# Program order of batches 0 to 2 redone, and zero matmuls of up to 512 columns in place of several of 128

## The chip, the cores and the metric

The kernel runs on one core of a Trainium2 chip. The metric is the device time of one execution in microseconds (us). A profiled execution has a span some 1.8 us shorter than its timed value; spans are compared with spans only.

## The reference

A retention layer (attention without softmax, with a decay by distance) feeds a two-layer network with the tanh form of GELU. There are 8 batches, 8 heads, 576 positions and 64 values a head; the network is 512 by 2048 by 512 over 4608 tokens.

```python
def _attn_ref(q, k, v):
    scale = 1.0 / np.sqrt(D_)
    scores = scale * np.matmul(q, k.transpose(0, 1, 3, 2))
    gamma = 1.0 - 2.0 ** (-5.0 - np.arange(H))
    Dmat = np.where(rel >= 0, gamma[:, None, None] ** rel[None], 0.0)   # rel = i - j
    return np.matmul(scores * Dmat[None], v)

def _moe_ref(x, w_in, w_out):
    h = x @ w_in
    g = 0.5 * h * (1.0 + np.tanh(c * (h + 0.044715 * h * h * h)))
    return g @ w_out
# ... x is the retention output, transposed to (tokens, heads * values)
```

## The kernel before

The retention is worked out in chunks of 128 positions, two to a "pair" of chunks. For each (batch, pair, head half) the kernel loads fp32 tiles of q, k and v, casts them to fp16, transposes q and k on TensorE (`tr`), makes scores (`score_mm`), masks them on VectorE (`mask_sc`), transposes a rescaled key back (`back`), makes the state of the chunk (`state_mm`), carries it along on VectorE (`scan`), casts it (`put`), and adds inner and carried parts in PSUM, the banks that TensorE's products are written to (`values`, `inter_mm`), which `evac` writes as the input of the network. `up` and `up_half` make the first network product; `down` makes the second.

```python
    def tr(b, s, hh, i, eng):                 # q or k: four PE transposes, then a copy
        a = att[b]
        t = bank("tr", F16)
        pad(("tr", b, s, hh, i), t)
        for g in range(4):
            nc.tensor.transpose(t[:, 128 * g : 128 * g + 128], a["kq"][:, s, hh, i, 128 * g : 128 * g + 128], ident)
        # ... copies to a["T"] by eng; S2 means half on ScalarE, half on VectorE

    def back(b, s, hh, eng):
        # ... four transposes of a["T"] into t
        copy(eng, a["kq"][:, s, hh, 0, :], t[:, 0:512])

    def put(b, n, eng, hhs=(0, 1)):           # two casts of a state
        # ...
        for hl in range(2):
            e = (A, V)[hl] if eng is S2 else eng
            copy(e, tbd[b % 2][half[hl], n, qs, half[hl]], w[half[hl], qs])
```

Zero matmuls are put ahead of real ones. Their products are never used, since the real matmul that follows overwrites the bank; they keep TensorE from standing still.

```python
    def pad(key, t, o=0):
        for _ in range(pads.pop(key, 0)):
            if t.dtype == F16:
                nc.tensor.transpose(t[:, 0:128], wz[:, 0:128], ident)
            else:
                nc.tensor.matmul(t[:, o : o + 128], wz[:, 0:128], wz[:, 0:128], start=(o == 0), stop=True, skip_group_check=True)
```

The order of all this is fixed by hand. `units` is a list of 79 pieces of work for batches 0 to 2: units 0 to 9 are empty, 10 on are the network's products. `plan` lists (unit, step) pairs; after each unit its steps are emitted in the order of the list. Each engine gets its own instructions in that order, so a step that stands early on an engine holds up all later ones of that engine. In both kernels q and k of batch 0 are cast to a layout of four-token tiles (the set `R4`), so this is not part of the difference.

```python
    def run(units, plan):
        for i, f in enumerate(units):
            f()
            for step in plan.get(i, ()):
                step()
    # ...
    units = [L(int) for _ in range(10)] + [L(F0.up_half, j, 1) for j in (0, 1)] + [L(int)] * 2 + [L(F0.up, f) for f in range(4, NF)]
    units += [L(F1.up_half, j, u) for u in range(2) for j in range(NJ)]
    units += [L(F.down, m) for F in (F0, F1) for m in MS]
    units += [L(F2.up, f) for f in range(NF)] + [L(F2.down, m) for m in MS]
    plan = add({},
        # ...
        (5, L(put, 0, 1, A)),                 # state cast on ScalarE
        # ...
        (6, L(put, 0, 0, A)),                 # state cast on ScalarE
        # ...
        (7, L(back, 0, 1, 1, A)),             # the kq copy that the second half of the state product waits for
        # ...
        (6, L(cast_w_in, 0, 3, A)),           # weight cast on ScalarE, unit 6: ahead of back in unit 7
        # ...
    )
```

Of the kernel before, what the change touches and what calls it, by code (L numbers as in the profile page):

```python
# [12 lines left out]
F32 = mybir.dt.float32  # L13
# [6 lines left out]
def kernel(  # L20
# [124 lines left out]
    def pad(key, t, o=0):  # L145
        for _ in range(pads.pop(key, 0)):
            if t.dtype == F16:
                nc.tensor.transpose(t[:, 0:128], wz[:, 0:128], ident)
            else:
                nc.tensor.matmul(t[:, o : o + 128], wz[:, 0:128], wz[:, 0:128], start=(o == 0), stop=True, skip_group_check=True)  # L150
# [140 lines left out]
    def load_w_in(g, ct, home=None):  # L291
        load_w(("i", g, ct), moe_w_in[128 * ct : 128 * ct + 128, 512 * g : 512 * g + 512], home)
# [592 lines left out]
    def add(plan, *entries):  # L885
# [16 lines left out]
    load_qkv(0, 0, 1, "q", None)  # L902
    load_qkv(0, 1, 1, "q", None)
    load_qkv(0, 1, 1, "k", None)
    load_qkv(0, 0, 1, "v", None)
    load_qkv(0, 0, 0, "v", None)
    load_w_in(0, 3, E)
    load_qkv(0, 1, 0, "v", None)
    load_qkv(0, 1, 1, "v", None)
    load_w_in(0, 2, E)  # L910
    load_w_in(0, 1, E)
    load_w_in(0, 0, E)
    load_w_in(1, 1, E2)
    load_w_in(1, 0, E2)
    load_w_in(1, 3, E2)
    load_w_in(2, 1, None)
    load_w_in(2, 2, None)
    load_qkv(1, 0, 0, "k", None)
    load_w_in(1, 2, E2)
    load_qkv(1, 0, 1, "q", None)  # L920
# [3 lines left out]
    load_qkv(1, 0, 1, "k", None)  # L924
    load_qkv(1, 0, 0, "v", None)
    load_w_in(3, 3, None)
    load_w_in(3, 1, None)
    load_w_in(3, 2, None)
    load_w_in(3, 0, None)
    load_qkv(1, 0, 1, "v", None)  # L930
    load_qkv(1, 1, 1, "q", O)
    load_qkv(1, 1, 0, "q", O)
    load_qkv(1, 1, 0, "k", O)
    load_qkv(1, 1, 1, "k", O)
    load_w_out(0, None)
    load_qkv(1, 1, 0, "v", O)
    load_qkv(1, 1, 1, "v", O)
    load_w_out(1, None)
    load_w_out(6, E3)
    load_w_out(2, None)  # L940
    load_w_out(4, E3)
    load_w_out(3, None)
    load_w_out(5, E3)
    load_w_out(14, H)
    load_w_out(8, O)
    load_w_out(10, H)
    load_w_out(7, E3)
    load_w_out(12, H)
    load_w_out(9, O)
    load_w_out(11, H)  # L950
    load_w_out(15, H)
    load_qkv(2, 1, 1, "q", None)
    load_qkv(2, 1, 0, "k", None)
    load_w_out(13, H)
    load_qkv(2, 0, 0, "q", None)
    load_qkv(2, 0, 0, "k", None)
    load_qkv(2, 1, 0, "q", None)
    load_qkv(2, 0, 0, "v", None)
    load_qkv(2, 0, 1, "q", None)
    load_qkv(3, 0, 1, "k", None)  # L960
    load_qkv(2, 0, 1, "v", None)
    load_qkv(2, 0, 1, "k", None)
    load_qkv(2, 1, 1, "k", None)
    load_qkv(2, 1, 1, "v", None)
    load_qkv(2, 1, 0, "v", None)
    load_tail(0)
    load_qkv(3, 0, 0, "q", None)
    load_qkv(3, 0, 0, "v", None)
# [8 lines left out]
    load_qkv(3, 1, 1, "q", None)  # L977
    load_tail(2)
    load_qkv(3, 1, 1, "v", None)


    pads.update({
        ("tr", 0, 1, 0, 0): 8,
        ("tr", 0, 1, 1, 0): 0,
        ("tr", 0, 1, 1, 1): 0,
        ("st", 0, 1, 0): 1,
        ("st", 0, 1, 1): 8,
# [4 lines left out]
        ("us", 0, 0): 2,  # L992
        ("us", 0, 1): 8,
        ("xs", 0, 0): 5,
        ("xs", 0, 1): 0,
        ("in", 0, 3): 0,
        ("tr", 0, 0, 0, 0): 7,
        ("tr", 0, 0, 0, 1): 11,
# [5 lines left out]
        ("tr", 0, 1, 0, 1): 6,  # L1004
        ("in", 0, 1): 10,
# [8 lines left out]
    def turn():  # L1014
# [8 lines left out]
        (0, L(cast_qk, 0, 0, 0, "q", A)),  # L1023
        (0, L(cast_qk, 0, 0, 0, "k", V)),
        (1, L(new_x, 0)),
        (0, L(cast_qk, 0, 1, 0, "q", V)),
        (0, L(tr, 0, 0, 0, 0, V)),
        (0, L(cast_qk, 0, 1, 0, "k", A)),
        (0, L(mask)),
        (1, L(tr, 0, 0, 0, 1, V)),  # L1030
        (1, L(tr, 0, 1, 0, 0, V)),
        (2, L(score_mm, 0, 0, 0)),
        (2, L(mask_sc, 0, 0, 0)),
        (2, L(back, 0, 0, 0, V)),
        (1, L(tr, 0, 1, 0, 1, S2)),
        (3, L(score_mm, 0, 1, 0)),
        (0, L(cast_qk, 0, 0, 1, "k", A)),
        (2, L(cast_qk, 0, 0, 1, "q", G)),
        (3, L(back, 0, 1, 0, A)),
        (3, L(tr, 0, 1, 1, 1, V)),  # L1040
        (2, L(tr, 0, 0, 1, 0, S2)),
        (2, L(tr, 0, 0, 1, 1, A)),
        (1, L(cast_qk, 0, 1, 1, "q", G)),
        (3, L(mask_sc, 0, 1, 0)),
        (5, L(back, 0, 0, 1, A)),
        (1, L(cast_qk, 0, 1, 1, "k", G)),
        (3, L(tr, 0, 1, 1, 0, A)),
        (4, L(score_mm, 0, 0, 1)),
        (4, L(mask_sc, 0, 0, 1)),
        (5, L(state_mm, 0, [0])),  # L1050
        (3, L(cast_v, 0, 0, 0, G)),
        (5, L(scan, 0, 0)),
        (3, L(cast_v, 0, 0, 1, G)),
# [3 lines left out]
        (6, L(mask_sc, 0, 1, 1)),  # L1057
# [3 lines left out]
        (7, L(back, 0, 1, 1, A)),  # L1061
        (8, L(inter_mm, 0, 0, 1)),
        (8, L(evac, 0, 0, 1)),
        (7, L(cast_v, 0, 1, 1, V)),
        (7, L(cast_v, 0, 1, 0, G)),
        (5, L(evac, 0, 0, 0)),
        (7, L(state_mm, 0, [1])),
        (7, L(scan, 0, 2)),
        (7, L(put, 0, 2, S2)),
        (8, L(inter_mm, 0, 1, 1)),  # L1070
        (8, L(inter_mm, 0, 1, 0)),
        (7, L(values, 0, 1)),
        (9, L(cast_w_in, 0, 2, G)),
        (9, L(evac, 0, 1, 0)),
# [4 lines left out]
        (6, L(cast_w_in, 0, 3, A)),  # L1079
        (8, L(cast_w_in, 0, 1, G)),  # L1080
        (8, L(cast_w_in, 0, 0, G)),
        (12, L(put, 0, 3, A)),
        (9, L(F0.up_half, 0, 0)),
# [4 lines left out]
        (7, L(cast_w_in, 1, 0, A)),  # L1088
        (10, L(cast_w_in, 2, 1, A)),
        (7, L(cast_w_in, 1, 3, A)),  # L1090
        (12, L(F0.mix_sc, 0, 2, V)),
        (8, L(cast_w_in, 1, 1, A)),
        (9, L(cast_w_in, 2, 2, V)),
        (7, L(turn)),
        (12, L(F0.mix_sa, 0, 2, V)),
        (9, L(cast_w_in, 2, 0, V)),
        (7, L(cast_w_in, 1, 2, A)),
        (19, L(F0.mix_sc, 2, 2, V)),
        (17, L(cast_qk, 1, 0, 1, "q", V)),
        (10, L(cast_qk, 1, 0, 0, "q", A)),  # L1100
        (18, L(F0.mix_d, 0, 2, V)),
        (15, L(tr, 1, 0, 0, 0, S2)),
        (18, L(cast_w_in, 3, 0, A)),
        (19, L(tr, 1, 0, 1, 1, A)),
        (15, L(tr, 1, 0, 1, 0, V)),
        (19, L(F0.mix_sa, 2, 2, G)),
        (19, L(score_mm, 1, 0, 0)),
        (22, L(mask_sc, 1, 0, 1)),
        (17, L(cast_w_in, 3, 2, G)),
# [3 lines left out]
        (21, L(cast_v, 1, 0, 1, G)),  # L1113
        (19, L(cast_w_in, 3, 1, A)),
        (20, L(F0.mix_d, 2, 2, V)),
        (21, L(new_x, 1)),
        (20, L(cast_v, 1, 0, 0, G)),
        (19, L(mask_sc, 1, 0, 0)),
        (21, L(score_mm, 1, 0, 1)),
        (22, L(state_mm, 1, [0])),  # L1120
        (14, L(cast_w_in, 3, 3, G)),
        (24, L(cast_qk, 1, 1, 0, "k", V)),
# [3 lines left out]
        (27, L(cast_qk, 1, 1, 1, "q", A)),  # L1126
        (22, L(values, 1, 0)),
        (29, L(put, 1, 1, A)),
        (21, L(cast_qk, 1, 1, 0, "q", A)),
        (25, L(cast_v, 1, 1, 0, V)),  # L1130
        (25, L(tr, 1, 1, 0, 0, V)),
        (27, L(F0.mix_sc, 4, 2, G)),
        (23, L(evac, 1, 0, 1)),
        (22, L(evac, 1, 0, 0)),
        (24, L(cast_qk, 1, 1, 1, "k", A)),
        (26, L(cast_v, 1, 1, 1, V)),
        (28, L(tr, 1, 1, 1, 1, A)),
        (24, L(F0.mix_sa, 4, 2, V)),
        (27, L(tr, 1, 1, 0, 1, A)),
# [3 lines left out]
        (30, L(mask_sc, 1, 1, 0)),  # L1143
        (31, L(mask_sc, 1, 1, 1)),
        (28, L(score_mm, 1, 1, 0)),
        (29, L(score_mm, 1, 1, 1)),
        (32, L(inter_mm, 1, 1, 1)),
        (29, L(scan, 1, 2)),
        (29, L(put, 1, 2, A)),
        (30, L(mix_w_out, 0, "sums", G)),  # L1150
        (31, L(values, 1, 1)),
        (31, L(mix_w_out, 0, "sub", V)),
        (41, L(mix_w_out, 3, "add", G)),
        (31, L(inter_mm, 1, 1, 0)),
        (28, L(mix_w_out, 1, "copy", A)),
        (33, L(mix_w_out, 1, "add", G)),
        (33, L(mix_w_out, 2, "sums", G)),
        (32, L(mix_w_out, 1, "sums", G)),
        (33, L(evac, 1, 1, 1)),
        (32, L(mix_w_out, 3, "sub", V)),  # L1160
        (32, L(evac, 1, 1, 0)),
        (33, L(mix_w_out, 2, "add", V)),
        (41, L(mix_w_out, 7, "add", V)),
        (37, L(mix_w_out, 3, "sums", V)),
        (37, L(mix_w_out, 3, "copy", A)),
        (37, L(mix_w_out, 1, "sub", V)),
        (35, L(mix_w_out, 0, "copy", A)),
        (33, L(mix_w_out, 2, "copy", A)),
        (36, L(mix_w_out, 0, "add", V)),
        (36, L(mix_w_out, 4, "sums", G)),  # L1170
        (34, L(mix_w_out, 2, "sub", V)),
        (37, L(mix_w_out, 6, "sums", V)),
        (43, L(mix_w_out, 4, "add", G)),
# [384 lines left out]
```

## Time and profile before

| | before |
|---|---|
| time, median of 4 runs (range) | 301.67 us (301.43 to 303.33) |
| span of the profiled execution | 299.3 us |
| instructions; matmuls of TensorE | 8979; 3775 |
| TensorE busy | 289.3 us (97%) |
| first network product (`hp`, 256 columns) | 24.45 us |

Timelines give start, duration, engine, line and operation, with the idle time of the engine just before in brackets and what ended it. I use four marks on TensorE's timeline in all kernels, since between them the same work is done: the first `hp` product of 256 columns (start of the network of batch 0), the first `my` product (its second layer), the first `hp` product of batch 2, and the first `my` product of batch 3. For the kernel before they stand at 24.45, 59.73, 92.75 and 143.02 us, and TensorE ends at 295.93. The stretches between the first three marks hold units 10 to 55; the last stretch holds units 56 to 78 and the first network product of batch 3. This table by stretch of the kernel before has the columns: stretch, length, busy time (instructions) of TensorE, its weight loads, VectorE, ScalarE and GpSimd, then granted clock, DMA share, GB/s.

```profile
24.45:59.73 35.28, 34.76 (x447) 24.97 (x445) 31.45 (x58) 31.49 (x69) 22.29 (x21) 1.00 0.96 287
59.73:92.75 33.02, 32.97 (x574) 28.30 (x572) 31.33 (x62) 18.70 (x40) 13.73 (x18) 1.00 0.82 206
92.75:143.02 50.27, 49.48 (x708) 30.54 (x707) 41.97 (x80) 31.26 (x60) 17.35 (x20) 1.00 0.95 233
```

The reader is to see the difference between length and TensorE's busy time: 0.52, 0.05 and 0.79 us. All three stretches are bound by TensorE; 1.36 us is all that can be won after the start.

### The profile page before, as it was taken

What the parts mean: (1) busy time and instruction counts of PE and PEld (TensorE: products, weight loads), DVE (VectorE), ACT (ScalarE), POOL (GpSimd) and SP (SyncE); (2) the same over time, 40 slices, a digit from 0 to 9 for tenths busy, and PEclk for the clock granted to TensorE, in tenths of its full rate; (3) what the DMA queues carried; (4) which work ended last, traced back from release to release, by engine and by line L of the source; (5) the groups of instructions that cost most, each with busy time, mean ns of one, the idle gap of its engine ahead of it and who ended that gap; (6) DMA issues with size and microseconds to landing.
All of it is one profiled execution on the core that took longest, in us unless ns stands there. A gap on an engine that the chain in (4) does not pass through costs nothing.

```text
span 299.3 us, 8979 instructions
## 1 busy us (share of the span) xinstructions
PE 289.3 (97%) x3775; PEld 210.3 (70%) x3775; DVE 234.4 (78%) x450; ACT 167.9 (56%) x328; POOL 97.5 (33%) x128
## 2 busy tenths in 40 slices
PE   7879999999999999999999999999999999999995
PEld 6757467888886558745875587558754886787684
DVE  3786989989998897798567756799778298886774
ACT  7448969984474782465535653565445317614830
POOL 4651687545240054084035104699100000000000
PEclk9999999999999999999999999999999999999999
DMA  6998999659979999996997799663030003002204
GB/s 219 336 358 263 313 375 313 182 139 227 231 223 206 264 285 173 273 310 103 194 291 219 106 198 282 193 120 39 8 136 1 2 0 143 0 2 70 72 0 140
DMA packets 92663, 52.48 MB, mean 175 GB/s; under 512 B 38352, under 2 KB 86480, under 8 KB 92624
## 3 DMA queue, kind: packets, MB, share of 16 engines
q1 hardware_dynamic: 92288, 51.26, 64.7%
q10 hardware_dynamic: 336, 0.66, 0.8%
q8 instruction: 29, 0.48, 0.7%
q14 instruction: 10, 0.08, 0.1%
HBM read 36.70 MB, written 9.44 MB: 154 GB/s over the span
## 4 chain that ended last, share of the span: by engine, by line
PE 81%; DVE 8%; ACT 7%; DMA 2%; issue 1%; SPq 0%; DVEq 0%; ACTq 0%
PE hp L635 26%; PE my L777 10%; PE mz L777 9%; PE mu L777 5%; PE mv L777 5%; PE mw L777 5%; PE hp L721 5%; ACT tbd L241 2%; PE py L665 2%; DVE ret L445 2%; PE xs L574 2%; PE xs L547 2%; PE st L432 2%; DMA ld<-in_q_dram 2%; ACT gT L639 1%; DVE ws L520 1%
## 5 line engine op out<-in xcount | busy, mean ns | idle before, releaser
L635 PE MATMUL hp<-x,w_in_sb 128*128 128x512 f16 x400 | 92.1, 379 | 0.6 <-ACT gT L639 0.5
L639 ACT ACTIVATE gT<-hp 128x512 f16<-128x512 f32 x108 | 63.6, 596 | 42.2 <-PE hp L635 41.5
L635 PEld LDWEIGHTS <-w_in_sb 128*128 128x128 f16 x432 | 40.9, 98 | 43.5 <-issue 1.0
L777 PEld LDWEIGHTS <-gT 128*128 128x128 f16 x576 | 55.8, 98 | 8.1 <-ACT gT L708 0.2
L445 DVE TENSOR_TENSOR ret<-st,cm 128x512 f16<-128x512 f32 x64 | 40.0, 681 | 4.1 <-PE st L432 4.1
L241 POOL CAST kq<-ld 128x512 f16<-128x512 f32 x26 | 20.8, 801 | 64.7 <-DMA ld<-in_k_dram 32.2
L241 ACT CAST tbd<-ws 64x256 f16<-64x256 f32 x63 | 25.4, 403 | 24.4 <-DVE ws L520 23.8
L254 POOL TENSOR_TENSOR cv<-ld,sc 128x512 f16<-128x512 f32 x28 | 30.2, 1090 | 26.6 <-DMA ld<-in_v_dram 22.7
L777 PE MATMUL my<-w_out_sb,gT 128*128 128x256 f16 x288 | 34.5, 273 | 0.0
L777 PE MATMUL mz<-w_out_sb,gT 128*128 128x256 f16 x288 | 34.4, 273 | 0.0
L777 PEld LDWEIGHTS <-gsum 128*128 128x128 f16 x288 | 27.9, 98 | 3.4
L746 DVE TENSOR_TENSOR gsum<-gT 128x1024 f16<-128x1024 f16 x35 | 28.0, 800 | 2.2 <-ACT gT L727 1.7
L750 DVE TENSOR_TENSOR gT<-gT 128x1024 f16<-128x1024 f16 x36 | 27.7, 787 | 0.1
L587 DVE TENSOR_TENSOR x<-xs,gx 128x512 f16<-128x512 f32 x32 | 21.7, 684 | 5.5 <-PE xs L574 5.3
L804 DVE TENSOR_TENSOR ost<-ost,mv 128x512 f32<-128x512 f32 x18 | 11.6, 683 | 13.5 <-issue 9.4
L738 DVE TENSOR_TENSOR gdia<-gT 128x512 f16<-128x512 f16 (+1 forms) x33 | 18.0, 544 | 4.9 <-ACT gT L708 2.5
L721 PE MATMUL hp<-x,w_in_sb 128*128 128x256 f16 x160 | 18.7, 273 | 0.0
L241 ACT CAST kq<-ld 128x512 f16<-128x512 f32 x28 | 17.0, 616 | 2.5 <-DMA ld<-in_k_dram 1.3
L777 PE MATMUL mu<-w_out_sb,gsum 128*128 128x256 f16 x144 | 17.2, 273 | 0.0
L777 PE MATMUL mv<-w_out_sb,gsum 128*128 128x256 f16 x144 | 17.2, 273 | 0.0
L777 PE MATMUL mw<-w_out_sb,gdia 128*128 128x256 f16 x144 | 17.2, 273 | 0.0
L721 PEld LDWEIGHTS <-w_in_sb 128*128 128x128 f16 x160 | 15.2, 98 | 1.9
(117 smaller groups left out, 393.1 us busy)
## 6 DMA issues: line engine op xcount, KB each, us to landing
ld<-in_k_dram SPq DMA_DIRECT2D x30, 256.0 KB, 5.1
ld<-in_q_dram SPq DMA_DIRECT2D x30, 256.0 KB, 5.3
ld<-in_v_dram SPq DMA_DIRECT2D x30, 256.0 KB, 5.4
out_dram<-ost SPq DMA_DIRECT2D x14, 512.0 KB, 4.3
loan<-in_moe_w_out_dram SPq DMA_DIRECT2D x12, 256.0 KB, 5.4
loan<-in_moe_w_in_dram SPq DMA_DIRECT2D x8, 256.0 KB, 6.1
ld<-in_moe_w_in_dram SPq DMA_DIRECT2D x8, 256.0 KB, 6.1
ld<-in_moe_w_out_dram SPq DMA_DIRECT2D x4, 256.0 KB, 6.5
```

The source lines that it names most:

```text
L241: (eng.copy if eng is nc.scalar else eng.tensor_copy)(out=out, in_=in_)
L254: eng.tensor_tensor(out=unperm(att[b]["v"][:, s, hh, :]), in0=perm(t), in1=sc[:, 8 * hh : 8 * hh + 8] .rearrange("p (r h) -> p r h", r=2) ...
L445: nc.vector.tensor_tensor(out=x.rearrange("p (a m) -> p a m", a=2), in0=st[hl].rearrange("p (a m) -> p a m", a=2), in1=cm.rearrange("p r s ...
L587: nc.vector.tensor_tensor(out=xb[b][:, :, 2 * s + c].rearrange("p s q i -> p q s i"), in0=att[b]["x", s][c].rearrange("p (q s i) -> p q s ...
L635: nc.tensor.matmul(hp, w_in_sb[:, ct, 128 * f : 128 * f + 128], x[:, :, ct, :], start=(ct == 0), stop=(ct == 3),)
L639: nc.scalar.activation(out=self.g(f // 2)[:, f % 2], in_=hp, func=AF.Gelu_apprx_tanh)
L721: nc.tensor.matmul(hp[:, 256 * h : 256 * h + 256], w_in_sb[:, ct, 256 * j + 128 * h : 256 * j + 128 * h + 128], xb[self.b][:, :, 2 * u : 2 ...
L738: e.tensor_tensor(out=self.sa[:, j : j + n], in0=g[:, :, 0, 0:256], in1=g[:, :, 1, 256:512], op=ALU.add)
L746: e.tensor_tensor(out=self.sc[:, j : j + n], in0=g[:, :, 0], in1=g[:, :, 1], op=ALU.add)
L750: e.tensor_tensor(out=g.rearrange("p j h c -> p j (h c)")[:, :, 256:768].rearrange("p j (h c) -> p j h c", h=2), in0=g[:, :, :, 0:256], in ...
L777: nc.tensor.matmul(t[u] if isinstance(t, list) else t[:, 256 * u : 256 * u + 256], lhs(j, slice(128 * u, 128 * u + 128)), w_out_sb[:, j, w ...
L804: nc.vector.tensor_tensor(out=out, in0=in0, in1=t, op=op)
```

## The change

The intent: fewer waits in the first 25 us by another order of the steps on each engine, smaller corrections of order later, and nearly the same columns of zero matmuls (132 units of 128 columns for 127) in fewer instructions. The core of the diff (cut):

```diff
     def pad(key, t, o=0):
-        for _ in range(pads.pop(key, 0)):
-            if t.dtype == F16:
-                nc.tensor.transpose(t[:, 0:128], wz[:, 0:128], ident)
-            else:
-                nc.tensor.matmul(t[:, o : o + 128], wz[:, 0:128], wz[:, 0:128], start=(o == 0), stop=True, skip_group_check=True)
+        n = pads.pop(key, 0)
+        t = t.bitcast(F32) if t.dtype == F16 else t
+        while n > 0:
+            m = min(n, (512 - o) // 128)
+            nc.tensor.matmul(
+                t[:, o : o + 128 * m],
+                wz[:, 0:128],
+                wz[:, 0:128].unsqueeze(1).to_broadcast([128, m, 128]),
+                start=(o == 0), stop=True, skip_group_check=True,
+            )
+            n -= m
 # ... loads in another order
-    load_qkv(0, 1, 1, "q", None)
     load_qkv(0, 1, 1, "k", None)
+    load_qkv(0, 1, 1, "q", None)
 # ... zero matmuls in units of 128 columns, e.g.
-        ("st", 0, 1, 1): 8,
+        ("st", 0, 1, 1): 12,
-        ("us", 0, 1): 8,
+        ("us", 0, 1): 4,
 # ... start
-        (3, L(back, 0, 1, 0, A)),
-        (3, L(tr, 0, 1, 1, 1, V)),
-        (2, L(tr, 0, 0, 1, 0, S2)),
-        (2, L(tr, 0, 0, 1, 1, A)),
+        (3, L(tr, 0, 1, 1, 1, S2)),
+        (2, L(back, 0, 1, 0, A)),
+        (1, L(tr, 0, 0, 1, 0, S2)),
+        (3, L(tr, 0, 0, 1, 1, A)),
-        (7, L(cast_v, 0, 1, 1, V)),
+        (6, L(cast_v, 0, 1, 1, G)),
-        (6, L(cast_w_in, 0, 3, A)),
+        (7, L(cast_w_in, 0, 3, A)),
-        (12, L(put, 0, 3, A)),
+        (11, L(put, 0, 3, V)),
-        (7, L(cast_w_in, 1, 0, A)),
+        (7, L(cast_w_in, 1, 0, V)),
 # ... some 150 further moves of (unit, step) pairs up to unit 78, such as
-        (24, L(F0.mix_sa, 4, 2, V)),
+        (22, L(F0.mix_sa, 4, 2, G)),
-        (78, L(put, 4, 0, A)),
+        (78, L(put, 4, 0, S2)),
```

In the list of the changed kernel `cast_w_in(0, 3)` stands behind `back(0, 1, 1)` within unit 7, so the copy now comes first on ScalarE.

## The prediction

> **What bounds the kernel now.** I read the page's busy table first: TensorE is busy 289.3 of 299.3 us, so all that program order can recover is the 10 us in which it is idle and whatever it does that is not wanted. The 40-slice view says where that lies.
>
> ```profile
> PE   7879999999999999999999999999999999999995
> ...
> DMA  6998999659979999996997799663030003002204
> ```
>
> TensorE falls below nine tenths only in the first three slices (7.5 us each) and in the last. The last slice is the drain of the output, in code that the diff does not touch. So the change is decided in the first 25 us. The table by stretch (engine busy time, then granted clock, DMA share, GB/s) cuts them up.
>
> ```profile
> 7.20:12.26 5.06, 3.78 (x72) 3.53 (x72) 4.66 (x12) 0.89 (x2) 2.04 (x4) 1.00 1.10 328
> 12.26:16.61 4.35, 4.35 (x110) 3.50 (x107) 3.10 (x8) 2.74 (x7) 4.35 (x7) 1.00 1.08 366
> 19.60:21.76 2.16, 0.00 (x1) 0.00 (x1) 1.64 (x3) 2.06 (x5) 0.65 (x1) 1.00 1.09 340
> 45.00:59.73 14.73, 14.55 (x217) 12.21 (x215) 14.49 (x28) 14.25 (x35) 9.55 (x9) 1.00 0.88 247
> ```
>
> The stretch 19.60 to 21.76 holds no TensorE work at all; in 45 to 60 us TensorE, VectorE and ScalarE are all above 96%. The TensorE timeline around the hole:
>
> ```profile
> 18.71 0.61 PE L150 MATMUL us<-wz 128*128 128x128 f16 x8
> 19.25 0.32 PE L500 MATMUL us<-cv,kq 64*64 64x64 f16 x16
> 21.76 0.32 PE L500 MATMUL us<-cv,kq 64*64 64x64 f16 x16 [2.19 <-ACT kq L241]
> ...
> 24.45 3.66 PE L721 MATMUL hp<-x,w_in_sb 128*128 128x256 f16 x32
> ```
>
> Half of the state product of the second pair of chunks runs at 19.25, and the other half waits 2.19 us for a ScalarE copy of `kq`. The first product of the feed-forward block (L721) starts at 24.45, and from there TensorE is nearly unbroken: its idle time from 24.45 to 92.75 sums to 0.58 us, and one gap of 0.51 us follows at 127. **The kernel is a start-up chain of 24.45 us followed by a TensorE-bound body.** The ScalarE timeline says why the copy was late:
>
> ```profile
> 15.67 0.58 ACT L241 COPY kq<-tr 128x512 f16<-128x512 f16 x1 [0.72 <-PE tr L415]
> 18.93 1.65 ACT L241 CAST tbd<-ws 64x256 f16<-64x256 f32 x4 [2.68 <-DVE ws L520]
> 20.60 0.62 ACT L241 CAST w_in_sb<-loan 128x512 f16<-128x512 f32 x1
> 21.13 0.58 ACT L241 COPY kq<-tr 128x512 f16<-128x512 f16 x1
> ```
>
> Its transposes were done near 18.87, but ahead of it in program order stand four state casts, which waited until 18.93 for VectorE's scan, and a weight cast. VectorE was late because the scan (17.04) stands behind four masks of 0.60 us (14.73 to 17.12 in the chain of work).
>
> **What the skill says.** "TensorE: Matmul & The Clock Gate", Part 1, says the ScalarE and VectorE queues are strict FIFO; the ScalarE lines above agree. Its section "Back-to-back issue gap" gives N/2.4 + 2.5 ns for a warm matmul. The trace agrees: sixteen 256-column matmuls take 1.75 us, 109 ns each; 512 columns take 216 ns (1.73 us for eight). Part 4 says a PE transpose does not count as busy for the clock gate as a matmul does, a possible reason for turning zero transposes into zero matmuls. But the trace shows no cold clock after 4.25 us: the warm-up's 256-column matmuls take 210 ns, while real transposes come at 55 ns (0.22 us per four) from 4.7 us on and the first 32 of L721 run at 109 ns each. "PSUM — Partial Sum Buffer", the four PSUM rules, limits one output to a bank of 512 fp32 columns, which is what the new helper fills.
>
> **The change, part by part.** *Zero matmuls.* Before: 60 zero transposes and 67 zero matmuls of 128 columns, 127 units. After: the table sums to 132 units, in some 45 instructions. The largest group of 23 transposes takes 1.28 us in the chain; as five of 512 and one of 384 columns it is 5 x 216 + 162 = 1.24 us. All other groups change by -0.2 to +0.25 us. The columns stay, so the effect by itself is about nothing (within 0.2 us). Fewer instructions save no array time.
>
> *Start-up order.* I replay the new order by hand with the durations of the before trace (kq cast 0.43 on VectorE, quarter-tile copy 0.335, mask 0.60, scan 0.35 to 0.45, state cast 0.405 each, back copy 0.50 to 0.58, pad unit 0.054).
> - The tile q(0,1,0) still lands at 7.17 and is the first fixed point. VectorE now copies the first transpose before it (5.1 us instead of 7.63), so it has 0.67 us less to do after 7.2.
> - TensorE: the 23 pads move ahead of the first scores. tr(0,0,1,0) then runs at 9.2 rather than 12.1, first scores at 10.05, second scores at 10.96 instead of 12.97.
> - The q(0,1,1) cast on GpSimd ends near 10.8; the remaining transposes run at 11.3, 11.9, 12.1. ScalarE carries five of their six copies until 13.45, so the scores of (0,0,1) start at 13.5 instead of 14.48.
> - VectorE's two masks of (0,1,0) finish at 13.5 and the last pair at 15.05. **The four masks no longer queue up**: before they ended at 17.12. The two v casts on GpSimd end at 14.1 (v still lands near 12.0), in time.
> - State at 14.3 to 15.1, scans to 16.3, state casts on ScalarE 16.35 to 18.0, and then directly the back copy, since the weight cast now follows it: 18.0 to 18.5. The waiting half of the state product runs at 18.55 instead of 21.76, 3.2 us earlier (about 2.6 from the earlier scan, 0.6 from the weight cast).
> - Scan and last state cast 18.95 to 20.25; inter products with 18 pad units 19.45 to 21.1; VectorE then casts w_in(1,0) and evacuates by 21.15. The first feed-forward product starts at about 21.2 instead of 24.45: **-3.2 us**, my estimate with an error of about 0.8.
>
> *Body, units 10 to 55.* The same PE work in almost the same order, so the shift carries through if inputs follow. Moved to GpSimd: one mix_sa (1.25 us on VectorE; a like sum took 2.17 on GpSimd), a k cast. Moved to VectorE: a v cast (0.68), w_in(1,0) (0.42), put(0,3) (0.58), w_out sums and add (0.75 + 0.41). VectorE gains a net 1 us in a part where it has 3.8 us idle (24.45 to 59.73) and only 0.24 us from 45 on. I allow **+0.6 us** given back.
>
> *Units 56 to 78.* Of eight state casts two move from ScalarE to VectorE (ScalarE 0.82 us lighter), where the before trace has eight of them in a row (122.88 to 126.86) delaying a GELU and TensorE by 0.51 us. I allow **-0.3 us**. F2's mix_d on GpSimd is in a part with GpSimd mostly idle: nothing.
>
> Sum: 0 - 3.2 + 0.6 - 0.3 = -2.9; 301.9 - 2.9 = 299.0 us.
>
> **Rivals.** (1) *DMA takes the place of the wait.* For: its share is 1.05 to 1.14 from 5 to 25 us, and bytes do not arrive sooner because VectorE is quicker. To 45 us some 14.0 MB were moved (six slices of 7.5 us at 219, 336, 358, 263, 313, 375 GB/s); 3 us earlier means 333 GB/s instead of 311, while the best slice made 375. Against: at 22 to 26 us the queue waited 3.1 us for a slot to be freed by VectorE's weight cast, so part of supply moves with the chain. One exposed point: w_in(1,0) is now cast ahead of the evacuation, lands near 19.6 by my count and is wanted at 20.15. If it holds: about 300.7. (2) *VectorE or ScalarE become the bound at 45 to 60 us.* For: both above 96%. Against: they shift with TensorE and the stage is no shorter, and the w_out sums are wanted only by the sixth and seventh products. If it holds: 300 to 301. (3) *The reorder is worth nothing*, because pads were hiding other waits and the last-landing tiles bind: 301.9. Against: the tiles of batch 0 were all cast by 15.03, but for one v tile that waited its turn on VectorE until 20.56, so they had landed. (4) *The program speeds up beyond the start* as the whole search was redone: TensorE idle after 24.45 before the drain is under 2 us, so at most 297.
>
> **Range and chances.** The replay's error (0.8) and the rivals give 297.3 to 301.0, leaning on the slow side of the centre. Faster by over 2% needs 295.9, that is 6.0 us, nearly all of the 6.6 us in which TensorE is idle before 280 us, and 1.05 of those precede the first matmul: 0.03. Slower by over 2% needs new waits of 9 us: 0.01. Within 2%: 0.96.
>
> **What would show it.** The first L721 at 20.5 to 22 us; the 2.19 us wait for ScalarE's kq copy gone or under 0.7; the first four masks in two pairs ending near 15; no new TensorE idle over 1 us in 22 to 92 us; DMA share still near 1. TensorE busy time as before within 0.5 us. I am wrong if the first L721 is early and the end is not (rivals 1, 2: new waits at 30 to 75 us), or if a tile's landing holds the first scores.

## The result, and the profile after

The changed kernel took 298.37 us (median of 4 runs, 297.70 to 299.20) against 301.67 us, a ratio of 0.988 (95% interval 0.984 to 0.992): within 2%, inside the predicted range, 0.6 us under the predicted centre. A ratio is here the mean time of one kernel's fast runs over that of the other's fast runs of the same rounds, so it is not quite the ratio of the medians quoted. Executions over 1.5% slower than the fastest of the same kernel are left out of the means. Run again twice beside other kernels, the changed kernel had medians of 298.42 and 298.85 us with ratios of 0.989 and 0.991.

The page of the changed kernel, its head, TensorE's slices and the DMA's slices:

```profile
span 295.9 us, 8809 instructions
...
PE   8989999999999999999999999999999999999995
...
DMA  6999999677789969995896999482120002002204
```

The span fell by 3.4 us. TensorE's first four slices read 8, 9, 8, 9 where they read 7, 8, 7, 9; DMA stays at nine tenths or above from the second slice to the seventh, as predicted. TensorE is busy for 289.5 us (289.3 before), with 86 matmuls fewer.

TensorE's timeline of the changed kernel around the hole of before:

```profile
17.70 0.32 PE L506 MATMUL us<-cv,kq 64*64 64x64 f16 x16
18.92 0.32 PE L506 MATMUL us<-cv,kq 64*64 64x64 f16 x16 [0.90 <-ACT kq L247]
19.07 0.62 PE L553 MATMUL xs<-ret,cv 64*64 64x128 f16 x32
...
21.73 3.44 PE L727 MATMUL hp<-x,w_in_sb 128*128 128x256 f16 x30
```

The same half of the state product waits for the same copy, but 0.90 us instead of 2.19, and the first network product is at 21.73 instead of 24.45. ScalarE's timeline of the changed kernel says what is left of the wait:

```profile
16.61 1.65 ACT L247 CAST tbd<-ws 64x256 f16<-64x256 f32 x4 [2.07 <-POOL tbd L133]
18.28 0.59 ACT L247 COPY kq<-tr 128x512 f16<-128x512 f16 x1
20.27 0.40 ACT L247 CAST tbd<-ws 64x256 f16<-64x256 f32 x1 [1.40 <-DVE ws L526]
20.58 1.13 ACT L247 CAST w_in_sb<-loan 128x512 f16<-128x512 f32 x2
```

The weight cast is now behind the copy; four state casts are still ahead of it. They start at 16.61 instead of 18.93. The bracket names GpSimd's clearing of `tbd` as what came last, but in the profile of changed_again below it names the scan. In the three profiles of the changed kernel the casts start 0.51 us after the start of the scan's last step (16.10, 16.69 and 16.61 us), wherever the clearing stands, so the scan is what counts. Why it is earlier, VectorE's timelines show, first of the kernel before, then of the changed one:

```profile
14.65 2.47 DVE L445 TENSOR_TENSOR ret<-st,cm 128x512 f16<-128x512 f32 x4
17.04 0.41 DVE L520 TENSOR_TENSOR ws<-us,gt 128x256 f32<-128x256 f32 x1
```

```profile
12.28 2.58 DVE L451 TENSOR_TENSOR ret<-st,cm 128x512 f16<-128x512 f32 x4
15.11 0.42 DVE L526 TENSOR_TENSOR ws<-us,gt 128x256 f32<-128x256 f32 x1 [0.24 <-PE us L506]
```

The row of four masks is still a row of four. It was not broken up; it merely begins 2.4 us earlier, and so the scan (`ws`) begins 1.9 us earlier. The three stretches of the changed kernel, marks at 21.73, 56.43, 89.65 and 139.60, TensorE's end at 292.52:

```profile
21.73:56.43 34.70, 34.52 (x445) 24.85 (x444) 29.98 (x59) 31.07 (x67) 16.86 (x18) 1.00 1.05 311
56.43:89.65 33.22, 33.12 (x575) 28.54 (x573) 31.93 (x65) 18.60 (x39) 14.28 (x18) 1.00 0.83 202
89.65:139.60 49.95, 49.44 (x708) 30.43 (x707) 44.17 (x82) 29.71 (x57) 19.71 (x22) 1.00 0.95 231
```

The stretches took 34.70 for 35.28, 33.22 for 33.02 and 49.95 for 50.27 us. With the start's 2.72 the sum is -2.72 - 0.58 + 0.20 - 0.32 = -3.42 us. After the last mark both kernels take 152.9 us, to 0.01. The changed kernel was profiled twice more (changed_again, changed_third), and its spans were 296.5 and 297.5 us: one profile of it is not good for more than a microsecond.

### The profile page after: what moved, and what is told of

It reads as the page before. It is cut to its first block, busy times and chain, and to the rows that moved or that the text cites. A ratio compares the mean times of both kernels' runs of the same rounds, so it can differ in the third digit from the quotient of the medians.

```text
span 295.9 us, 8809 instructions
## 1 busy us (share of the span) xinstructions
PE 289.5 (98%) x3689; PEld 206.7 (70%) x3689; DVE 236.7 (80%) x455; ACT 165.7 (56%) x323; POOL 96.9 (33%) x129
## 4 chain that ended last, share of the span: by engine, by line
PE 74%; DVE 8%; ACT 6%; DMA 4%; POOL 3%; issue 2%; SPq 1%; DVEq 0%; POOLq 0%; ACTq 0%
PE hp L641 26%; PE my L783 9%; PE mz L783 8%; PE hp L727 5%; PE mv L783 5%; PE mu L783 5%; PE mw L783 4%; PE py L671 2%; ACT tbd L247 2%; PE xs L580 2%; DMA ld<-in_v_dram 2%; DMA ld<-in_moe_w_in_dram 2%; PE xs L553 2%; DVE ost L810 2%; POOL cv L260 2%
## 5 line engine op out<-in xcount | busy, mean ns | idle before, releaser
L260 POOL TENSOR_TENSOR cv<-ld,sc 128x512 f16<-128x512 f32 x28 | 30.8, 1114 | 35.4 <-DMA ld<-in_v_dram 22.4
L247 POOL CAST kq<-ld 128x512 f16<-128x512 f32 x27 | 18.0, 673 | 58.1 <-DMA ld<-in_k_dram 46.6
L247 ACT CAST tbd<-ws 64x256 f16<-64x256 f32 x59 | 23.7, 402 | 22.8 <-DVE ws L526 19.8
L756 DVE TENSOR_TENSOR gT<-gT 128x1024 f16<-128x1024 f16 x35 | 28.4, 830 | 0.2
L247 ACT CAST kq<-ld 128x512 f16<-128x512 f32 x27 | 16.3, 616 | 2.5 <-DMA ld<-in_q_dram 1.5
```

What stands on the lines that cost most here:

```text
L247: (eng.copy if eng is nc.scalar else eng.tensor_copy)(out=out, in_=in_)
L260: eng.tensor_tensor(out=unperm(att[b]["v"][:, s, hh, :]), in0=perm(t), in1=sc[:, 8 * hh : 8 * hh + 8] .rearrange("p (r h) -> p r h", r=2) ...
L756: e.tensor_tensor(out=g.rearrange("p j h c -> p j (h c)")[:, :, 256:768].rearrange("p j (h c) -> p j h c", h=2), in0=g[:, :, :, 0:256], in ...
```

## The experiments

**Theory:** the gain is made of the new order before the first `hp` (about 2.5 us), plus a few tenths from the moves in the later units; the zero matmuls' width is worth nothing by itself. **Rival one:** the moves of the later units need the earlier start, or spoil it. **Rival two:** one move, the weight cast behind the copy, does most of it. **Rival three:** the fewer, wider zero matmuls do it, through the clock or through the number of instructions. Twelve kernels ran, in three sets of four; each set shares a chip and runs of the kernel before, whose medians were 301.17, 301.66 and 300.96 us. All were correct. "Marks" below are those of the stretches. Each kernel had six timed runs, the kernel before eleven in each set. Without its slow run the first median would be 300.98.

One caution for all comparisons of the start: the tile k(0,1,0) lands a little differently in every execution. Its transposes ran at 7.10 us in the profile of before, 6.82 after, and 6.72 to 7.88 in the others. Where the start matters, I also give the time from these transposes to the first `hp`: 17.35 us before, 14.91 after.

A second caution: the granted clock. The profile of before shows 1.00 throughout, but 14 of the 32 fast runs of that kernel in the three sets have a mean granted clock of 0.992 to 0.994. They took 302.1 us on average, the other 18 took 300.8. About 3.4 us at half clock in 300 us give a mean of 0.994, and the profiles of rest_only and w03_after_back below show just that, near 22 us. Such runs were 4 of 6 in pads_only, pads_again, rest_only and w03_after_back, 2 of 6 in narrow_pads, and none of 16 of the changed kernel and none of 24 in start_only, puts_after_back, queues_undone and queues_freed. When the others of these runs lost it was not traced; in the two profiles it follows idle time of TensorE. So a part of the timed gain is that the changed kernel does not lose the clock. Without such runs of the kernel before, changed_again gains 3.05 us by means instead of 3.39, and changed_third 1.85 instead of 2.66.

### pads_only: the new helper alone

```diff
# the kernel before, with its order and its table of zero matmuls, and
-        for _ in range(pads.pop(key, 0)):          # one instruction for each 128 columns
+        # the changed kernel's pad(): one instruction for up to 512 columns
```

> Before's order and before's table of zero matmuls, with only the helper changed: zero matmuls of up to 512 columns in place of several of 128 (and in place of zero transposes). Start theory: no change, within 0.3 us of before (301.4 to 302.0), first L727 at 24.45 within 0.2 us, because the zero columns stay the same. Rival (wide zero matmuls are themselves the gain): at least 1 us faster, first L727 at 23.5 or earlier.

Measured: 303.15 us against 301.17, ratio 1.008 (1.004 to 1.012), granted clock 1.00 throughout in the profile. This is no gain, rather a loss of about 2 us. The profile, with a span 1.9 us longer than before, has two causes for it. The tile landed late in this execution (transposes at 7.88), and from there to the first `hp` it took 17.26 us, as in the kernel before (17.35): the start is unchanged, late only with its tile. The rest is far away. TensorE's timeline of this kernel near 283 us, its ScalarE timeline a little earlier, and ScalarE's line of the kernel before:

```profile
283.11 0.60 PE L671 MATMUL py<-xf,wf 128*128 128x256 f16 x4 [0.93 <-DVE q L690]
```

```profile
279.38 2.32 ACTq L834 DMA_DIRECT2D out_dram<-ost  x3
```

```profile
278.48 1.38 ACTq L828 DMA_DIRECT2D out_dram<-ost  x3
```

Issuing three output stores from ScalarE's queue took 2.32 us instead of 1.38. The copy behind them was late, and TensorE stood 0.93 us. The packet records of the trace show what was special: one of the three took 1.37 us instead of 0.43, and in that time (279.72 to 280.87) a packet of the DMA queue of kind "instruction" moved. The repeat, pads_again, shows the same (1.48 us, packet from 278.54 to 279.78). In the twelve other profiles no such packet moved while these stores were issued, and each took 0.38 to 0.44 us. After the last mark this kernel needs 153.85 us, 0.94 more than before.

### start_only: the new order of units 0 to 9, with the new helper and table

```diff
# the changed kernel, with the plan of units 10 to 78 and the later loads of the kernel before, e.g.
-        (11, L(put, 0, 3, V)),
+        (12, L(put, 0, 3, A)),
-        (78, L(put, 4, 0, S2)),
+        (78, L(put, 4, 0, A)),
```

> Units 0 to 9 (all of batch 0 up to its first feed-forward product), the head of the load list, the helper and the table from the changed kernel; units 10 on from before. Start theory: first L727 at 21.7 and 2.5 to 3.0 us faster than before. Rival (the gain of the start is given back in the old body, where VectorE and ScalarE are above 96% busy and transfers come no sooner): first L727 at 21.7 but 1.5 us or less faster, with new TensorE waits between 25 and 60 us.

Measured: 299.04 us against 301.17, ratio 0.994 (0.991 to 0.997). The first `hp` stands at 22.12, 14.98 us after the tile, with a kq wait of 0.90. So the start alone has the start's whole gain in the trace. The stretches after it are those of the kernel before: 35.39, 32.87 and 50.23 us, with the wait of 0.5 us for a GELU near 127 still there (here at 125.17).

### rest_only: the later units alone

```diff
# the kernel before, with the plan of units 10 to 78 and the later loads of the changed kernel, e.g.
-        (12, L(put, 0, 3, A)),
+        (11, L(put, 0, 3, V)),
-        (78, L(put, 4, 0, A)),
+        (78, L(put, 4, 0, S2)),
```

> The mirror: units 0 to 9, helper and table of before, units 10 on and the rest of the load list from the changed kernel. If start and rest add up: 0.5 to 0.9 us faster than before, first L721 at 24.45, the wait of 0.5 us at 127 us gone. Rival (the new body only helps because it starts earlier, or costs time of its own as the prediction's +0.6 us had it): no gain or up to 0.6 us slower.

Measured: 302.47 us against 301.17, ratio 1.003 (0.999 to 1.007): nothing to see in the time. The stretches tell more. Here the first two:

```profile
25.76:60.45 34.69, 34.52 (x448) 24.89 (x446) 29.90 (x59) 30.10 (x65) 16.48 (x17) 1.00 0.97 289
60.45:94.70 34.25, 33.17 (x575) 28.43 (x572) 31.87 (x65) 18.65 (x39) 14.58 (x18) 1.00 0.76 201
```

The first stretch takes 34.69 us and the third 49.95, just as in the changed kernel (34.70 and 49.95). The gain of 0.3 us in the third belongs to the later moves and needs no earlier start: all nine profiles with the new later units take 49.95 or 49.96 us there, the five with the old ones 50.22 to 50.62. Rival one is out for it. The 0.6 us of the first stretch is less sure, since a third profile of the changed kernel took 35.31 us. Two losses hide these gains. In the second stretch TensorE waits 1.0 us for a cast on GpSimd, which no other profile with the new later units shows but that of narrow_pads. And the first `hp` came at 25.76, because TensorE's clock fell, as the table of single microseconds shows (columns as before):

```profile
20.00:21.00 1.00, 0.09 (x12) 0.00 (x0) 1.00 (x3) 0.96 (x3) 0.00 (x0) 1.00 0.79 237
...
23.00:24.00 1.00, 1.00 (x11) 1.00 (x12) 0.45 (x2) 0.80 (x2) 0.00 (x0) 0.50 1.17 297
```

After an idle time of 1.76 us, the granted clock was 0.50 from 22 to about 25.5 us.

### w03_after_back: one move of the start

```diff
# the kernel before, and
-        (6, L(cast_w_in, 0, 3, A)),     # ahead of the kq copy on ScalarE
         (7, L(back, 0, 1, 1, A)),
+        (7, L(cast_w_in, 0, 3, A)),
```

> Before, with one step moved: ScalarE's weight cast w_in(0,3) goes behind the copy of the transposed-back kq tile that TensorE waits for. Prediction's term: the wait of 2.19 us becomes 1.65, the first L721 comes 0.5 us earlier and the kernel is 0.5 us faster (0.3 to 0.6). Rival (the w_in cast then holds the first feed-forward product, or another wait takes its place): within 0.15 us of before.

Measured: 301.23 us against 301.17, ratio 1.000 (0.997 to 1.004). Rival two is out: the move alone is worth nothing that these runs show, and at most about 1 us by the interval. TensorE's timeline of this kernel:

```profile
20.50 0.32 PE L500 MATMUL us<-cv,kq 64*64 64x64 f16 x16 [1.19 <-DVE cv L254]
20.63 0.44 PE L547 MATMUL xs<-ret,cv 64*64 64x128 f16 x17
22.11 0.64 PE L547 MATMUL xs<-ret,cv 64*64 64x128 f16 x15 [1.03 <-issue]
22.68 1.25 PE L150 MATMUL us<-wz 128*128 128x128 f16 x10
```

The wait for the copy is gone, and three others take its place. First, the other operand, a v tile cast on VectorE, is now the last to come (1.19 us). Then TensorE stops for 1.03 us in the middle of a group of 32 like matmuls, with no semaphore to wait for ("issue"). Last, ten zero matmuls take 1.25 us where they took 0.73 in the kernel before (22.46): the granted clock was 0.50 from 22.0 to about 25.4 us, as in rest_only. The first `hp` came at 25.59, later than before.

### changed_again and narrow_pads: the changed kernel, and the same with narrow zero matmuls

```diff
# changed_again: the changed kernel, no edit
# narrow_pads: the changed kernel with the order and the table of the changed kernel, and
-        # pad() with one instruction for up to 512 columns
+        # pad() of the kernel before: a transpose or matmul for each 128 columns
```

> The changed kernel itself, as the yardstick for the three others on this chip. 2.5 to 3.7 us faster than before, as in its first rounds (0.9879); first L727 between 21.4 and 22.4, clock row without a slice below 9.

> The changed kernel with the old helper (each unit a 128-column zero transpose or zero matmul, the new table). If the width is worth nothing: within 0.3 us of the changed kernel. Rival from the run with wide ones alone, which was 0.8% slower than before: wide ones cost 2 us, so this is 1 to 2 us faster than the changed kernel. Rival that wide ones help hold the clock: 1 us or more slower, with a slice of the granted clock below 9.

Measured: changed_again 298.42 us against 301.66 (ratio 0.989, 0.986 to 0.992); narrow_pads 300.26 (0.996, 0.992 to 0.999), so 1.84 us slower by medians of the same set. Width is worth about half of the gain or more when the order is new. TensorE's wait list of narrow_pads (waiter, what it waited for, us in total, times, longest) has two items that no profile of the unedited changed kernel shows at that size:

```profile
PE xs L560 <- POOL cvt L272: 1.0, 1, 1.0
...
PE xs L547 <- issue: 0.8, 1, 0.8
```

Their sum is near the measured difference. The second lies, as in w03_after_back, within the 32 matmuls of `values`, after the 13th:

```profile
19.88 0.39 PE L547 MATMUL xs<-ret,cv 64*64 64x128 f16 x13
21.06 0.47 PE L547 MATMUL xs<-ret,cv 64*64 64x128 f16 x19 [0.80 <-issue]
```

The granted clock was 1.00 all through this profile, so the clock is not the reason for these two. (Two of the six timed runs did lose it; the other four average 299.87 us, still 1.60 above changed_again.) What remains is the count of instructions ahead of that point. In w03_after_back TensorE's stream up to it is that of the kernel before. The stop came after the 17th of the 32 there and after the 13th here, but in both profiles exactly 351 matmuls had run (`--windows 0:21.05` counts them in either trace). The profile lists a DMA queue of kind "instruction" with 29 packets and 0.48 MB in both kernels; with some 3700 matmuls and as many weight loads that is one packet for 254 to 260 of them, if TensorE's instructions are what it carries, which the profile does not say. By the packet records one such packet moved from 18.56 to 19.66 us here and from 19.47 to 20.66 in w03_after_back, and the stops ended 1.40 and 1.45 us after its end. In the kernel before the packet ended at 20.24, and the 352nd matmul, held by the kq wait, came at 22.14, late enough not to stop; in the changed kernel, with wide zero matmuls, it comes only at 27.06. So the stop looks like instructions that are not yet supplied, and fewer instructions move it out of the way. I had no run that changes the supply alone: two stops at the same count and the same delay are strong evidence, but not a test.

The first item, the GpSimd cast, is the third in a row behind a cast that waits for a q tile's load. That cast began, at its load's landing, 49.4 us after the first `hp` in narrow_pads and rest_only, and 47.6 to 49.0 us after it in the seven other profiles with the new later units (six of them with wide zero matmuls, one with none). Whether narrow zero matmuls make it land later, and how, stays open.

### no_pads: no zero matmuls at all

```diff
# the changed kernel, and
-    pads.update({ ... })
+    pads.clear()
```

> The changed kernel with no zero matmuls at all (the warm-up of 16 stays). Clock theory: TensorE is then idle for most of 5 to 20 us, the granted clock falls to 0.5 as it did for 3 us after the idle stretch at 20 to 22 us in two of the runs so far; the first L727 comes at 21 to 23.5 and the kernel is 0.5 to 2.5 us slower than the changed one. Rival (the zero matmuls stand in the way of real ones): first L727 0.5 to 1 us earlier and the kernel as much faster.

Measured: 299.69 us against 301.66, ratio 0.994 (0.992 to 0.997); 1.3 us slower than changed_again by medians. The page's row of the granted clock, and one row of the table by stretch:

```profile
PEclk9558999999999999999999999999999999999999
```

```profile
8.00:10.00 2.00, 1.58 (x23) 0.82 (x21) 1.99 (x6) 1.15 (x3) 0.61 (x1) 0.50 1.06 343
```

Without them TensorE runs at half clock from 8 to 24 us, with the first `hp` at 22.97. So the zero matmuls buy the clock, worth about 1.3 us here. Narrow ones give back as much in the new order: the runs of narrow_pads (299.08 to 301.49) and of no_pads (299.59 to 300.90) overlap, so that which of the two is slower is not shown.

### puts_after_back: taking the rest of the wait away

```diff
# the changed kernel, and
-        (5, L(put, 0, 1, A)),
-        (6, L(put, 0, 0, A)),
         (7, L(back, 0, 1, 1, A)),
+        (7, L(put, 0, 0, A)),
+        (7, L(put, 0, 1, A)),
```

> The changed kernel with the last ScalarE queueing removed: the copy of back(0,1,1) goes ahead of the four state casts put(0,0) and put(0,1), which are wanted only 2 us later. If ScalarE's order is what still holds the state product (0.90 us wait): the wait falls under 0.2 us, first L727 0.6 to 0.9 us earlier, 0.6 to 0.9 us faster than the changed kernel. Rival (the inter products or w_in casts then wait for ScalarE): within 0.3 us of the changed kernel.

Measured: 298.21 us, against 298.42 for changed_again, so the same. TensorE's and VectorE's timelines of this kernel:

```profile
18.50 0.32 PE L506 MATMUL us<-cv,kq 64*64 64x64 f16 x16 [0.27 <-ACT kq L247]
...
27.21 0.84 PE L361 MATMUL tr<-ident,kq 128*128 128x128 f16 x12 [0.34 <-DVE kq L247]
...
36.35 0.41 PE L553 MATMUL xs<-ret,cv 64*64 64x128 f16 x15 [0.39 <-DVE ret L451]
```

```profile
24.06 0.76 DVE L247 CAST w_in_sb<-ld 128x512 f16<-128x512 f32 x2 [1.23 <-DMA ld<-in_moe_w_in_dram]
```

The wait fell from 0.90 to 0.27 us. Of these 0.63 us the first `hp` shows little: it came 14.77 us after the tile instead of 14.91, since TensorE now waited 0.33 us for a state cast at 20.52. And the first stretch took 35.39 instead of 34.70, so more was given back than won. VectorE reached a weight cast before its load had landed, stood 1.23 us, and everything behind that cast came late, a k cast (27.21) and masks of batch 1 (36.35). The prediction's rival of DMA taking the place of the wait is real at this point, one step further on than the change went.

### changed_third and queues_undone: the two moves of the start undone together

```diff
# changed_third: the changed kernel, no edit
# queues_undone: the changed kernel, and
-        (6, L(cast_v, 0, 1, 1, G)),
+        (7, L(cast_w_in, 0, 3, A)),     # ahead of the kq copy on ScalarE again
         (7, L(back, 0, 1, 1, A)),
+        (7, L(cast_v, 0, 1, 1, V)),     # on VectorE again
-        (7, L(cast_w_in, 0, 3, A)),
```

> The changed kernel once more, as the yardstick on this chip: 2.5 to 3.7 us faster than before.

> The changed kernel with its two queue moves for the second half of the state product undone: weight cast w_in(0,3) again ahead of the kq copy on ScalarE, and the v cast (0,1,1) again on VectorE. The prediction split the start's gain into 2.6 us from the earlier scan and 0.6 us from the queue. If that split holds: the state product's wait is 1.4 to 1.5 us instead of 0.9, first L727 0.4 to 0.7 us later, kernel 0.4 to 0.7 us slower than the changed one. Rival (the queue moves carry the gain): 1.5 us or more slower. Rival (nothing, the order of the copies is hidden): within 0.15 us.

Measured: 298.85 us and 298.98 us against 300.96. The trace does show the two moves: the kq wait is 1.42 us, and the first `hp` comes 16.05 us after the tile instead of 14.91 to 15.00 in three profiles of the changed kernel.

```profile
19.68 0.32 PE L506 MATMUL us<-cv,kq 64*64 64x64 f16 x16 [1.42 <-ACT kq L247]
...
22.80 3.65 PE L727 MATMUL hp<-x,w_in_sb 128*128 128x256 f16 x32 [0.27 <-DVE x L593]
```

The time does not show them: 0.13 us by medians, in runs that spread over 1.7 us, so this is inconclusive. One reason is visible. The first stretch of changed_third took 35.31 us where two other profiles of the same kernel took 34.70; the changed kernel itself varies by 0.6 us there (queues_undone took 34.69).

### pads_again: pads_only once more

```diff
# pads_only, no further edit
```

> Repeat of the run with wide zero matmuls alone in the order of before, which was 0.8% slower (2.3 us) though its columns are the same; in its trace the loss was 0.7 us of a tile that landed late and 0.9 us of a late DMA issue on ScalarE near 280 us. If those were chance: within 0.5 us of before this time. If wide ones are bad in this order: 1.5 to 2.5 us slower again, with the same waits.

Measured: 302.05 us against 300.96, ratio 1.002 (0.998 to 1.005). With an ordinary landing of the tile (7.41), the first `hp` was at 23.90, 16.49 us after it. The loss near the end came again: three stores took 2.44 us to issue, in code that is the same as before and long after the last zero matmul (near 24 us), and TensorE stood 1.05 us near 282. It was in both profiles of this program and in none of the others. In the old order, then, wide zero matmuls gain nothing in the time; the start may gain up to 0.9 us, and 1.0 us is lost at 282, where the store met an instruction packet (see pads_only). That fewer instructions shift the packets, so that one falls on the store, fits both profiles but was not tested.

### queues_freed: four corrections together

```diff
# the changed kernel, and
-        ("in", 0, 2): 7,
+        ("in", 0, 2): 2,                       # fewer zero matmuls ahead of inter_mm
-        (5, L(put, 0, 1, A)),
-        (6, L(put, 0, 0, A)),
         (7, L(back, 0, 1, 1, A)),
+        (7, L(put, 0, 0, A)),                  # state casts behind the copy
+        (7, L(put, 0, 1, A)),
-        (7, L(cast_w_in, 1, 0, V)),
         (8, L(evac, 0, 0, 1)),
+        (8, L(cast_w_in, 1, 0, V)),            # weight cast behind the evacuation
-        (9, L(cast_w_in, 2, 0, V)),
-        (10, L(cast_w_in, 2, 2, V)),
         (12, L(cast_qk, 1, 0, 1, "k", V)),
+        (12, L(cast_w_in, 2, 0, V)),           # casts of late weights behind the k cast
+        (12, L(cast_w_in, 2, 2, V)),
```

> The changed kernel with four steps moved: the kq copy of (0,1,1) ahead of the state casts on ScalarE, the first evacuation of the second chunk ahead of the w_in(1,0) cast on VectorE, the casts of w_in(2,0) and (2,2) behind the cast of k(1,0,1) instead of ahead of the scan (in the first try VectorE stood 1.23 us waiting there for w_in(2,0) to land), and 2 zero units instead of 7 before the last inter product. If orders and not landings now hold TensorE: first L727 0.9 to 1.3 us earlier and 0.5 to 1.0 us faster than the changed kernel. Rival (transfers are the next bound, whatever the order): first L727 early, but within 0.3 us of the changed kernel, with TensorE waiting for casts of late tiles between 25 and 37 us.

Measured: 297.59 us (297.20 to 298.17) against 300.96, ratio 0.987 (0.983 to 0.991). It is the fastest of all, 1.07 us under changed_third by means of six runs each (297.68 and 298.75), with a 95% interval of about 0.3 to 1.8 us as I work it out from the spread of these runs. The first `hp` was at 21.28, 14.39 us after the tile, half a microsecond less than in the changed kernel. Part is again given back on VectorE, now at the masks of batch 1 alone:

```profile
35.64 0.21 PE L553 MATMUL xs<-ret,cv 64*64 64x128 f16 x1 [0.48 <-DVE ret L451]
36.24 0.41 PE L553 MATMUL xs<-ret,cv 64*64 64x128 f16 x15 [0.39 <-DVE ret L451]
```

Which of the four corrections carries the gain was not taken apart.

## Why the prediction was right or wrong

The time came out as predicted, and so did most of the mechanism. By the steps of the sum:

- **The start, -3.2 predicted, about -2.4 measured.** In the first profile it is -2.72, of which 0.28 is the tile's earlier landing; from the tile on, it is 17.35 - 14.91 = 2.44 us. In the two further profiles it is -2.12 and -2.20, and 2.4 us from the tile on. The cause is as named: an earlier scan and a weight cast behind the copy. Two readings inside the step were off. The four masks did not separate into two pairs; they stayed a row that begins 2.4 us earlier and ends near 14.9, where I had 15.05. And I put the 0.6 us down to the moved weight cast. In my replay the v cast was already on GpSimd, and w03_after_back shows that this was needed: without it the weight cast's move gains nothing, since the v cast on VectorE comes next. The two together are worth 0.5 us of the kq wait (1.42 against 0.91) and about 1.1 us of the start in queues_undone, in one profile. The replay was 0.3 us too early at the state casts and 0.5 at the first `hp` (predicted 16.35, 18.55 and 21.2; measured 16.61, 18.92 and 21.73).
- **Units 10 to 55, +0.6 predicted; -0.4, -0.4 and +0.7 measured** in the three profiles of the changed kernel (34.70 + 33.22, 34.70 + 33.23 and 35.31 + 33.70 us) against one profile of before (35.28 + 33.02). The sign stays open. In the first two the loss did not come: I let VectorE's added microsecond count against TensorE and left out that other moves in the same list take waits away. In the third TensorE waited twice, 0.3 us each, for VectorE's masks, the kind of loss that the term stood for. The first profile alone would have made the term look plainly wrong.
- **Units 56 to 78, -0.3 predicted, -0.32 measured**, and -0.3 again in rest_only, while start_only keeps the old length and the old wait near 127 us. All profiles of the changed kernel agree on it. This step held as worked out.
- **Zero matmuls, 0 predicted.** On the array that is right: TensorE's busy time moved by 0.2 us. As a statement of their effect it is wrong. In the new order narrow ones cost 1.84 us, of which the profile shows a stop of 0.8 us without a semaphore and a wait of 1.0 us at a GpSimd cast. In the old order the wide ones gain nothing. I costed instructions by the columns that they stream and not by their count; the 86 fewer matmuls are part of what makes the start's gain visible.
- **The clock, no term predicted.** I read from one profile that the kernel before keeps its clock. By their mean clocks 14 of 32 fast runs did not, and 0.3 and 0.8 us of the gain by means on two chips come from those runs.

In the first profile -2.4 - 0.3 (landing) - 0.4 - 0.3 is -3.4; the spans of the three profiles fell by 3.4, 2.8 and 1.8 us, and the timed medians of the three sets by 3.3, 3.2 and 2.1. The predicted -2.9 lies among them, and partly by luck: the start came out 0.8 us smaller than predicted, the loss in the body came in one profile of three, and the instruction count and the clock, which the sum did not have, add to the gain.

Of the rivals, DMA did not take over (share 1.05 in the first stretch, and that stretch shorter), nor did VectorE or ScalarE become the bound. That the reorder is worth nothing fell. The last rival, a program quicker beyond the start too, is right for the 0.3 us of units 56 to 78; for units 10 to 55 it is open. Of the signs listed, no new idle over 1 us came true, and so did the first `hp` at 20.5 to 22 us in the first profile (21.73), though not in the next two (22.33 and 22.25). The kq wait of "gone or under 0.7" did not: 0.90 us.

## What to carry to other kernels

When a wait is to be removed, list everything that the waiting instruction needs and when each would arrive: moving only the last one hands the wait to the next (here from a copy on ScalarE to a cast on VectorE, and then to a stop without any semaphore). Instructions that only fill time can cost by their number even where their columns are free, so try them few and wide; leaving them out can cost the clock. A queue's order is worth a term in the sum in both directions: before allowing a loss for work that an engine gains, look what else the same list takes away, and profile a kernel more than once before giving a sign to half a microsecond. The clocks of the timed runs are to be read too: a profile that shows none lost does not mean that none is.

## What the Trainium skill lacked or had wrong

- "TensorE: Matmul & The Clock Gate", Part 1, ties the half clock to an idle window of about 3.4 us. Here a gap of 1.76 us was followed by a granted clock of 0.50 (rest_only), and so were two gaps of 1.19 and 1.03 us with 33 small matmuls between (w03_after_back). A gap of 2.19 us in the kernel before was not. The half clock then lasted for about 3.4 us in both (22.0 to 25.4 or 25.5), which agrees with the length of the page's window; that one or two gaps of half its length or less can be enough, the page does not say. The mean clocks of 14 of the 32 fast runs of the kernel before fit such a fall too.
- The same page, Part 4, says that transposes do not count as busy as matmuls do. In the kernel before TensorE ran transposes alone from 4.25 to 7.92 us, more than a window of the page, and the granted clock stayed 1.00; narrow_pads, which has zero transposes again, also had 1.00 throughout in its profile, and lost some in two of six timed runs. Zero matmuls are not shown to be better for the clock.
- "Runtime: NRT & Kernel Launch", "Instruction fetch mechanics", says that an engine's instructions are fetched in blocks of 16 KiB while the program runs, and calls the cost of crossing a block mostly hidden. The 29 packets of the kind "instruction" have that size here (16384 bytes each, 0.48 MB in all). If the reading of narrow_pads is right, the cost is not always hidden: TensorE stopped for 0.80 and 1.03 us before its 352nd matmul, until 1.40 and 1.45 us after such a packet had ended.
- No page says why issuing a store should now and then take three times as long: ScalarE issued each of four stores in 0.38 to 0.44 us in twelve profiles, but one of them took 1.37 and 1.48 us in pads_only and pads_again, each time while an instruction packet moved, which delayed TensorE by 0.93 and 1.05 us.
